# Decoding float64 weights with one VectorE operation fewer a half tile, the sign taken in by ScalarE, and the order planned with another TensorE rate

## The chip, the cores and the metric

One core of one Trainium2 chip runs the whole program. The metric is the device time of one execution in microseconds. Three executions of the kernel before took 681.01, 682.85 and 683.84 us; their median, 682.85 us, is the time that a change is measured against.

## The reference, cut to what matters

```python
def _attn_ref(q, k, v):                                  # 4 batches, 12 heads, 448 rows, 64 columns, float32
    scores = scale * np.matmul(q, k.transpose(0, 1, 3, 2))
    scores = np.where(mask, -1000000000.0, scores)       # causal
    scores = scores - np.max(scores, axis=-1, keepdims=True)
    attn = np.exp(scores)
    attn = attn / (np.sum(attn, axis=-1, keepdims=True) + 1e-09)
    return np.matmul(attn, v).astype(np.float32)

def _moe_ref(x, w_in, w_out):                            # x: 1792 x 768; w_in: 768 x 2048; w_out: 2048 x 768
    h = x @ w_in
    g = np.where(h >= 1, h, np.where(h <= -1, 0.0, (h + 1) ** 2 / 4.0))
    return (g @ w_out).astype(np.float32)
```

The attention's output, heads side by side, is the x of the two products behind it. The weights w_in and w_out arrive as float64: each is two 32-bit words, and the chip must make a float32 of them before TensorE can use it.

## The kernel before, in words

The work has three parts. **Attention** goes by 24 pairs of heads (4 batches of 6). For a pair, q and k are loaded and transposed on VectorE (line 446); scores are made on TensorE (lines 562, 567, 571); VectorE masks and takes the row bound (583); ScalarE takes the exponential (587); the rows are divided by their sum (510 to 513, GpSimd, ScalarE or VectorE); TensorE transposes them (525), and ScalarE copies them out (546); TensorE multiplies by v (612). **mlp1** makes h = x @ w_in for a batch of 448 rows and one of 16 blocks f of 128 columns, in 18 matmuls (line 405: 6 blocks of the sum, 3 passes of high and low parts); then comes the activation, written as min(r, 1) * max(h, r) with r = relu(h/2 + 1/2): ScalarE (414), VectorE (417), VectorE (419). The result goes to a scratch in HBM. A batch's blocks can be finished when all six pairs of that batch are done. **mlp2** reads the scratch back, splits it in high and low parts (325, 334), and makes the output in tiles of 128 rows with 3 passes for each block f (line 703).

The weights are decoded in halves of 128 x 384 weights by `decode` (line 341): 32 halves of w_in, then 32 of w_out, two for each f. The words of a half are loaded by SP's queue (line 360). The upper word, read as a float32, is multiplied by 2^-112, which moves the exponent's offset so that three bits can be dropped (line 361 on ScalarE, or line 363 on GpSimd); VectorE shifts it left by 3 (366), ors in the top three bits of the lower word (368), and ors in the sign bit of the upper word (371), which the shift has pushed out. The finished float32 is split: the high part is a rounding copy to the matmul's format (325, 327 or 326 on ScalarE, GpSimd or VectorE), the low part is the difference (334 or 335, GpSimd before VectorE). The buffer `wm` in which this happens has two slots, and a slot comes free when the low part of the half has been made. Weights share 16 slots `w`; w_out takes a slot when batch 3 of mlp1 has used that block of w_in.

The order of the instructions on each engine is not written by hand. `Plan.run` (line 105) simulates the engines, task by task, with a cost for each (lines 199 to 216, and `Clock` for TensorE, line 173): of the tasks that can start it takes the earliest, and among those on one engine the one of lower priority number. Where a task lists several engines, another one than the first is taken only if it would finish earlier than the first, counting what is queued on that (lines 125 to 134). `Clock.run` costs a matmul of n columns at n / 2.4 ns when TensorE is warm. The program is emitted in the order that the plan comes to, so a changed cost can move any instruction of the program. Attention has priority 13 for each pair (line 648), the decoding of block f of w_in has 80 + 3 f (line 645), mlp1's matmuls come behind all attention (line 654).

Of the kernel before, what the change touches and what calls it, by code (L numbers as in the profile page):

```python
# [10 lines left out]
F32 = mybir.dt.float32  # L11
F32R = mybir.dt.float32r
U32 = mybir.dt.uint32
ACTF = mybir.ActivationFunctionType
ALU = mybir.AluOpType
W_SHIFT = 2.0 ** -112


class Buf:
# [21 lines left out]
class Plan:  # L41
# [18 lines left out]
    def task(self, alts, prio, reads=(), writes=(), after=()):  # L60
        t = Task(alts, prio)
        for b, k in reads:
            w, rs = b.keys.setdefault(k, [None, []])
            if w is not None:
                t.deps.add(w)
            rs.append(t)
        for b, k in writes:
            w, rs = b.keys.setdefault(k, [None, []])
            if w is not None:
                t.deps.add(w)  # L70
            t.deps.update(r for r in rs if r is not t)
            b.keys[k] = [t, []]
        for b in {id(x): x for x, _ in (*reads, *writes)}.values():
            if not b.tasks and b.tag is not None:
                t.allocs.append(b)
            elif b.tasks and b.tag is not None:
                t.soft.add(b.tasks[0])
            b.tasks.append(t)
        t.deps.update(after)
        t.deps.discard(t)  # L80
        t.soft -= t.deps
        t.n_left = len(t.deps) + len(t.soft)
        for d in t.deps | t.soft:
            d.next.append(t)
        t.no = len(self.tasks)
        self.tasks.append(t)
        return t
# [85 lines left out]
class Clock:  # L173
# [7 lines left out]
    def run(self, t, matmuls):  # L181
        for n, m, rows, beside in matmuls:
            warm = self.cols.get(int(t / self.TICK) - 1, 0) >= self.ENOUGH
            d = max(m / 1.2, n / (2.4 if warm else 1.2)) / 1000 + (0.055 if beside else 0.002)
            a, z = int(t / self.TICK), int((t + d) / self.TICK)
            f = 1.0 if a == z else (z * self.TICK - t) / d
            self.cols[a] = self.cols.get(a, 0) + n * f * rows / 128
            self.cols[z] = self.cols.get(z, 0) + n * (1 - f) * rows / 128
            t += d
        return t  # L190


def mm(n, m=128, rows=128, times=1, pair=False):


    return [(n, m, rows, pair)] * times


def dve(n, fast=False):
    return ((n / 2 if fast else n) + 62) / 960  # L200


def act(n, extra=0.0):
    return n / 1200 + 0.055 + extra


def pool_ts(n, extra=0.0):
    return 0.83e-3 * n + 0.16 + extra


def pool_tt(n):
    return 2.08e-3 * n + 0.16


def dma(nbytes, rate=360.0):
    return nbytes / rate / 1000
# [3 lines left out]
def kernel(  # L220
# [9 lines left out]
    nc = tc.nc  # L230
    B, H, S, D = q.shape
# [24 lines left out]
    W2 = DM // 2  # L256
    scale = 1.0 / float(D) ** 0.5
# [29 lines left out]
    for z in range(2):  # L287
        nc.gpsimd.affine_select(
            out=mask[T * z:T * z + T, S - T:],
            in_=mask[T * z:T * z + T, S - T:],  # L290
# [9 lines left out]
        out=mask2[:, 2 * P:], in_=mask2[:, 2 * P:], pattern=[[-1, P]], compare_op=ALU.is_ge,  # L300
# [14 lines left out]
    task = plan.task  # L315

    def buf(tag, shape, dtype=F32):
        return plan.buf(tag, lambda: pools[tag].tile(shape, dtype, tag=tag, name=tag))

    def dma_task(out_fn, in_fn, cost, prio, **kw):  # L320
        return task([("SP", cost, lambda: nc.sync.dma_start(out=out_fn(), in_=in_fn()))], prio, **kw)  # L321
# [19 lines left out]
    def decode(w, c, src, prio, no):  # L341

        if no < 2 * (KF - NSTG):
            st, z = stages[no // 2 % NSTG], no % 2
            raw = lambda: st.tile.bitcast(U32)[:, z]
        else:
            st, z = buf("st", [P, 2 * S]), 0
            raw = lambda: st.tile.bitcast(U32)[:, :DM]
        m = buf("wm", [P, W2])

        def words(t):
            return raw().rearrange("p (c t) -> p c t", t=2)[:, :, t]

        def mu():
            return m.tile.bitcast(U32)

        hi = lambda: w[:, 0, c * W2:(c + 1) * W2]
        lo = lambda: w[:, 1, c * W2:(c + 1) * W2]
        dst, ap = src
        dma_task(lambda: dst(raw()), lambda: ap, dma(P * DM * 4), prio - 15, writes=[(st, (z, 0)), (st, (z, 1))])  # L360
        task([("ACT", act(W2, 0.04), lambda: nc.scalar.activation(
            out=m.tile, in_=words(1).bitcast(F32), func=ACTF.Copy, scale=W_SHIFT)),
              ("POOL", pool_ts(W2), lambda: nc.gpsimd.tensor_scalar(
            out=m.tile, in0=words(1).bitcast(F32), scalar1=W_SHIFT, scalar2=1.0, op0=ALU.mult, op1=ALU.mult))],
            prio, reads=[(st, (z, 1))], writes=[(m, 0)])
        task([("DVE", dve(W2, True), lambda: nc.vector.tensor_scalar(
            out=mu(), in0=mu(), scalar1=3, scalar2=None, op0=ALU.logical_shift_left))], prio, writes=[(m, 0)])
        task([("DVE", dve(W2), lambda: nc.vector.scalar_tensor_tensor(  # L368
            out=mu(), in0=words(0), scalar=29, in1=mu(), op0=ALU.logical_shift_right, op1=ALU.bitwise_or))],
            prio, reads=[(st, (z, 0))], writes=[(m, 0)])  # L370
        task([("DVE", dve(W2), lambda: nc.vector.scalar_tensor_tensor(  # L371
            out=mu(), in0=words(1), scalar=0x80000000, in1=mu(), op0=ALU.bitwise_and, op1=ALU.bitwise_or))],
            prio, reads=[(st, (z, 1))], writes=[(m, 0)])
        task(copy_alts(hi, lambda: m.tile, W2, "ACT POOL DVE"), prio, reads=[(m, 0)], writes=[(w, (0, c))])
        task(sub_alts(lo, lambda: m.tile, lambda: hi().bitcast(F32), W2, "POOL DVE"),
             prio, reads=[(m, 0), (w, (0, c))], writes=[(w, (1, c))])
# [21 lines left out]
    def mlp1(b, f, prio):  # L398
        h = buf("h", [P, 512])
        for kk in range(KD):  # L400
            x = XS[b, kk]

            def go(kk=kk, x=x):
                for n, (a, c) in enumerate(PASSES):
                    nc.tensor.matmul(  # L405
                        out=h[:, :S], lhsT=wi[f][:, a, kk * P:(kk + 1) * P], rhs=x[:, c],
                        start=(kk == 0 and n == 0), stop=(kk == KD - 1 and n == 2),
                    )

            task([("PE", mm(S, times=3), go)], prio,  # L410
                 reads=[(x, 0), (x, 1), (wi[f], (0, kk // K2)), (wi[f], (1, kk // K2))], writes=[(h, 0)])
        r, y = buf("r", [P, S]), buf("vv", [P, S])
        g0 = -1.0
        task([("ACT", act(S, 0.1), lambda: nc.scalar.activation(  # L414
            out=r.tile, in_=h[:, :S], func=ACTF.Relu, scale=0.5, bias=half[:, 0:1]))],
            g0, reads=[(h, 0)], writes=[(r, 0)])
        task([("DVE", dve(S), lambda: nc.vector.tensor_tensor(out=y.tile, in0=h[:, :S], in1=r.tile, op=ALU.max))],  # L417
             g0, reads=[(h, 0), (r, 0)], writes=[(y, 0)])
        task([("DVE", dve(S), lambda: nc.vector.scalar_tensor_tensor(  # L419
            out=r.tile, in0=r.tile, scalar=1.0, in1=y.tile, op0=ALU.min, op1=ALU.mult))],  # L420
            g0, reads=[(y, 0)], writes=[(r, 0)])
        dma_task(lambda: g_dram[f, :, b * S:(b + 1) * S], lambda: r.tile, dma(P * S * 4), g0,
                 reads=[(r, 0)], writes=[(gkeys, (f, b))])
# [222 lines left out]
    for b in range(B):  # L646
        for p in range(HP):
            prio = (b * HP + p) * 2 * HT
# [3 lines left out]
    for b in range(B):  # L652
        for f in range(KF):
            mlp1(b, f, 10000.0 + 1000 * b)
# [21 lines left out]
    for size in TILES:  # L676
        ts = list(range(tn, tn + size))
        t0, tn = tn, tn + size
        n = len(ts) * P
# [8 lines left out]
        for f in range(KF):  # L688
            prio = 6000.0 + t0 * 100 + f
# [3 lines left out]
                     prio, reads=[(gkeys, (f, b)) for b in bs], writes=[(raw, 0)], after=last)  # L693
            task(copy_alts(lambda gs=gs, n=n: gs[:, 0, :n], lambda raw=raw, n=n: raw[:, :n], n, "ACT POOL"), prio,
                 reads=[(raw, 0)], writes=[(gs, 0)])
            task(sub_alts(lambda gs=gs, n=n: gs[:, 1, :n], lambda raw=raw, n=n: raw[:, :n],
                          lambda gs=gs, n=n: gs[:, 0, :n].bitcast(F32), n, "DVE POOL"), prio,
                 reads=[(raw, 0), (gs, 0)], writes=[(gs, 1)])
            for t in ts:
# [9 lines left out]
                for steps in ([both[::2], both[1::2]] if f == KF - 1 else [both]):  # L709
                    task([("PE", mm(NO, times=len(steps)), lambda go=go, steps=steps: go(steps))],  # L710
                         20000.0 + t0 * 100 + f + 0.01 * t,
                         reads=[(gs, 0), (gs, 1)] + [(wo[f], x) for x in WK],
                         writes=[(acc[t, c], 0) for c in sorted({c for c, _ in steps})])
        for t in ts:
# [3 lines left out]
                out=ot[:, :NO], in_=a0[:, :NO], func=ACTF.Copy))], 0.0, reads=[(a0, 0)], writes=[(ot, 0)])  # L718
# [3 lines left out]
                out=ot[:, NO:cut], in_=a1[:, :cut - NO]))], 0.0, reads=[(a1, 0)], writes=[(ot, 1)])  # L722
            if final:
                task([("ACT", act(DM - cut), lambda ot=ot, a1=a1, cut=cut: nc.scalar.activation(
                    out=ot[:, cut:], in_=a1[:, cut - NO:NO], func=ACTF.Copy))], 0.0, reads=[(a1, 0)], writes=[(ot, 2)])
# [37 lines left out]
```

## Time and profile before

| | |
|---|---|
| median of three executions | 682.85 us (681.01 to 683.84) |
| the profiled execution, its own time | 683.23 us |
| its span, first to last instruction | 681.4 us |
| mean granted TensorE clock | 0.995 of full speed |

The profile shows one execution. Its own time is 1.8 us above its span and 0.4 us above the median. Times in the rows below are microseconds from the start of the span unless they say ns. PE is TensorE, DVE VectorE, ACT ScalarE, POOL GpSimd, SP the engine that issues all DMAs here. A busy matmul counts from its start to the end of its way through the array, so matmuls overlap in the records: the distance between starts tells how fast they go, and the busy time of an engine with short waits looks fuller than it is.

### The profile page before, as it was taken

How to read it: one execution, taken by the hardware profiler on the slowest of the kernel's cores; microseconds unless marked ns; L12 is line 12 of the kernel's file. 1: busy time of each engine (PE TensorE's matmuls, PEld its weight loads, DVE VectorE, ACT ScalarE, POOL GpSimd, SP SyncE). 2: the span in 40 equal slices, each digit the busy share in tenths (PEclk: the TensorE clock that was granted, in tenths of full speed). 3: DMA queues.
4: the chain of work that ended last, by engine and by line, in shares of the span. 5: the costliest groups of instructions: out<-in, count | busy, mean ns of one | idle time of the engine just before them, and what ended most of it. 6: DMA issues, size and time to landing. Idle time of an engine off the chain costs nothing.

```text
span 681.4 us, 11654 instructions
## 1 busy us (share of the span) xinstructions
PE 653.4 (96%) x3782; PEld 559.9 (82%) x3782; DVE 401.8 (59%) x922; ACT 314.0 (46%) x829; POOL 229.9 (34%) x369
## 2 busy tenths in 40 slices
PE   7988989898989999999999999999999999999997
PEld 3445767676767788777789789999999999999997
DVE  5667899999565666765665399887632112212221
ACT  3778766556556553775642544333422112111222
POOL 3257777676243333544330264353300000000000
PEclk8999999999989999999999999999999999999999
DMA  7668999985666666666674256566424212312312
GB/s 186 184 174 211 222 239 243 242 217 159 156 164 180 178 173 179 176 170 167 174 179 143 89 178 191 170 197 191 156 82 151 62 51 93 109 58 89 90 61 71
DMA packets 91900, 105.75 MB, mean 155 GB/s; under 512 B 34368, under 2 KB 75840, under 8 KB 91840
## 3 DMA queue, kind: packets, MB, share of 16 engines
q1 hardware_dynamic: 91840, 105.01, 56.2%
q8 instruction: 30, 0.49, 0.3%
q14 instruction: 30, 0.25, 0.1%
HBM read 67.35 MB, written 20.19 MB: 128 GB/s over the span
## 4 chain that ended last, share of the span: by engine, by line
PE 64%; DVE 12%; DMA 9%; issue 4%; POOL 3%; SPq 3%; ACT 3%; DVEq 0%; POOLq 0%; ACTq 0%
PE a L703 25%; PE h L405 16%; PE h L703 8%; PE t L612 5%; PE t L525 4%; SPq L321 3%; DMA st<-in_moe_w_out_dram 3%; DVE wm L368 3%; PE s L567 2%; DVE r L419 2%; DMA st<-in_k_dram 2%; PE s L562 2%; DVE wm L371 2%; DMA w<-in_moe_w_in_dram 2%; DMA st<-in_q_dram 1%
## 5 line engine op out<-in xcount | busy, mean ns | idle before, releaser
L405 PE MATMUL h<-x,w 128*128 128x448 f32 x1152 | 261.3, 372 | 2.6 <-POOL w L335 1.1
L405 PEld LDWEIGHTS h<-x,w 128*128 128x128 f32 x1152 | 209.2, 188 | 22.0 <-POOL w L335 2.3
L703 PE MATMUL a<-w,gs 128*128 128x384 f32 x1008 | 197.6, 334 | 0.0
L703 PEld LDWEIGHTS a<-w,gs 128*128 128x128 f32 x1008 | 176.8, 188 | 0.1
L334 DVE TENSOR_TENSOR gs<-gr,gs 128x512 fp32r<-128x512 f32 (+3 forms) x76 | 40.4, 532 | 137.5 <-ACT gs L325 137.5
L583 DVE CUSTOM_DVE_ANT_0 s<-s,mask 128x256 f32<-128x256 f32 (+6 forms) x168 | 73.0, 449 | 53.9 <-PE s L567 28.9
L325 ACT ACTIVATE gs<-gr 128x512 fp32r<-128x512 f32 (+3 forms) x79 | 39.2, 500 | 139.3 <-PE h L703 105.7
L587 ACT ACTIVATE e<-s,mn 128x256 f32<-128x256 f32 (+6 forms) x168 | 80.7, 487 | 40.2 <-DVE mn L583 36.5
L335 POOL TENSOR_TENSOR w<-wm,w 128x384 fp32r<-128x384 f32 x63 | 71.0, 1130 | 52.7 <-ACT w L325 51.1
L703 PE MATMUL h<-w,gs 128*128 128x384 f32 x336 | 80.8, 334 | 0.2 <-DVE vv L417 0.2
L510 POOL TENSOR_SCALAR e<-e,su 128x256 f32<-128x256 f32 (+5 forms) x103 | 64.1, 628 | 27.9 <-DVE su L598 19.3
L593 POOL TENSOR_SCALAR su<-su 128x2 f32<-128x2 f32 (+1 forms) x71 | 23.0, 325 | 135.7 <-ACT e L587 128.3
L525 PE MATMUL t<-ident,e 128*128 128x128 f32 x384 | 60.1, 281 | 8.8 <-POOL e L510 5.1
L546 ACT ACTIVATE pt<-t 128x384 f32<-128x384 f32 (+2 forms) x139 | 58.9, 464 | 19.0 <-PE t L525 18.2
L525 PEld LDWEIGHTS t<-ident,e 128*128 128x128 f32 x384 | 44.4, 142 | 26.2 <-POOL e L510 13.8
L703 PEld LDWEIGHTS h<-w,gs 128*128 128x128 f32 x336 | 60.2, 188 | 0.5 <-DVE vv L417 0.5
L414 ACT ACTIVATE r<-h,half 128x448 f32<-128x448 f32 x64 | 40.1, 630 | 39.1 <-PE h L405 38.5
L612 PE MATMUL t<-pt,vr 128*64 128x448 f32 (+3 forms) x384 | 52.0, 401 | 2.0 <-ACT pt L546 1.8
L417 DVE TENSOR_TENSOR vv<-h,r 128x448 f32<-128x448 f32 x64 | 39.5, 617 | 22.9 <-ACT r L414 22.7
L419 DVE SCALAR_TENSOR_TENSOR r<-r,vv 128x448 f32<-128x448 f32 x64 | 51.8, 810 | 0.9
L612 PEld LDWEIGHTS t<-pt,vr 128*64 128x64 f32 (+1 forms) x384 | 23.6, 138 | 34.4 <-issue 21.1
L446 DVE STREAM_TRANSPOSE qs<-st 128x448 f32<-128x448 f32 x48 | 46.3, 965 | 5.9 <-DMA st<-in_q_dram 3.4
(61 smaller groups left out, 563.2 us busy)
## 6 DMA issues: line engine op xcount, KB each, us to landing
g_scratch<-r SPq DMA_DIRECT2D x64, 224.0 KB, 2.2
st<-in_moe_w_out_dram SPq DMA_DIRECT2D x32, 384.0 KB, 3.2
w<-in_moe_w_in_dram SPq DMA_DIRECT2D x28, 384.0 KB, 5.2
st<-in_q_dram SPq DMA_DIRECT2D x96, 108.0 KB, 2.4
st<-in_k_dram SPq DMA_DIRECT2D x96, 108.0 KB, 2.6
q<-tt SPq DMA_DIRECT2D x76, 128.0 KB, 2.4
gr<-g_scratch SPq DMA_DIRECT2D x32, 256.0 KB, 2.7
k<-ks SPq DMA_DIRECT2D x76, 96.0 KB, 2.2
```

The lines of the kernel that those rows point to most:

```text
L334: "DVE": ("DVE", dve(n), lambda: nc.vector.tensor_tensor(out=dst(), in0=x(), in1=y(), op=op)),
L335: "POOL": ("POOL", pool_tt(n), lambda: nc.gpsimd.tensor_tensor(out=dst(), in0=x(), in1=y(), op=op)),
L405: nc.tensor.matmul(out=h[:, :S], lhsT=wi[f][:, a, kk * P:(kk + 1) * P], rhs=x[:, c], start=(kk == 0 and n == 0), stop=(kk == KD - 1 and n ...
L419: task([("DVE", dve(S), lambda: nc.vector.scalar_tensor_tensor(out=r.tile, in0=r.tile, scalar=1.0, in1=y.tile, op0=ALU.min, op1=ALU.mult)) ...
L446: task([("DVE", dve(S), lambda g=g, t=t: nc.vector.transpose(out=x[:, g].rearrange("p (r c) -> p c r", c=C), in_=t.tile.rearrange("p (c d) ...
L510: ("POOL", pool_ts(n, 0.09), lambda: nc.gpsimd.tensor_scalar(out=ev(), in0=ev(), scalar1=sc(), scalar2=1.0, op0=ALU.mult, op1=ALU.mult)),
L525: nc.tensor.transpose(t[:, c:c + P], es[i][:, j * P:(j + 1) * P], ident)
L546: task([("ACT", act(n), lambda: nc.scalar.activation(out=dst(), in_=src(), func=ACTF.Copy)), ("DVE", dve(n), lambda: nc.vector.tensor_copy ...
L583: task([("DVE", dve(n) + 0.01, lambda s=s, n=n, i=i: nc.vector.tensor_tensor_reduce(out=s[:, :n], in0=s[:, :n], in1=mask2[:, 3 * P - n:] i ...
L587: task([("ACT", act(n, 0.19), lambda s=s, n=n, i=i: nc.scalar.activation(out=es[i][:, :n], in_=s[:, :n], func=ACTF.Exp, scale=-1.0, bias=m ...
L612: nc.tensor.matmul(out=o[64 * g:64 * g + 64, j * P:S], lhsT=vr[:k, j, g, :], rhs=pt[:k, 7 * j:5 * j + NI, g, :], start=(j == 0), stop=(j = ...
L703: nc.tensor.matmul(out=acc[t, c][:, :NO], lhsT=gs[:, a, (t - t0) * P:(t - t0 + 1) * P], rhs=wo[f][:, z, c * NO:(c + 1) * NO], start=(f == ...
```

## The change

The scaling of the upper word becomes a Prelu on ScalarE with the same scale and a slope of 2^32 for negative words: these come out 2^32 times larger in magnitude, so the bit that the shift by 3 moves into the sign's place is set for them and clear for the others. The operation of line 371 is gone. The scaling can no longer go to GpSimd. In the plan, the or of line 368 costs 0.08 us more, a warm matmul n / 2.23 ns in place of n / 2.4 ns, and the last operation of the activation (419) may also go to GpSimd, there as two instructions.

```diff
--- before.py
+++ after.py
@@ -14,6 +14,7 @@
 ACTF = mybir.ActivationFunctionType
 ALU = mybir.AluOpType
 W_SHIFT = 2.0 ** -112
+W_SIGN = 2.0 ** 32
 
 
 class Buf:
@@ -181,7 +182,7 @@
     def run(self, t, matmuls):
         for n, m, rows, beside in matmuls:
             warm = self.cols.get(int(t / self.TICK) - 1, 0) >= self.ENOUGH
-            d = max(m / 1.2, n / (2.4 if warm else 1.2)) / 1000 + (0.055 if beside else 0.002)
+            d = max(m / 1.2, n / (2.23 if warm else 1.2)) / 1000 + (0.055 if beside else 0.002)
             a, z = int(t / self.TICK), int((t + d) / self.TICK)
             f = 1.0 if a == z else (z * self.TICK - t) / d
             self.cols[a] = self.cols.get(a, 0) + n * f * rows / 128
@@ -359,18 +360,13 @@
         dst, ap = src
         dma_task(lambda: dst(raw()), lambda: ap, dma(P * DM * 4), prio - 15, writes=[(st, (z, 0)), (st, (z, 1))])
         task([("ACT", act(W2, 0.04), lambda: nc.scalar.activation(
-            out=m.tile, in_=words(1).bitcast(F32), func=ACTF.Copy, scale=W_SHIFT)),
-              ("POOL", pool_ts(W2), lambda: nc.gpsimd.tensor_scalar(
-            out=m.tile, in0=words(1).bitcast(F32), scalar1=W_SHIFT, scalar2=1.0, op0=ALU.mult, op1=ALU.mult))],
+            out=m.tile, in_=words(1).bitcast(F32), func=ACTF.Prelu, scale=W_SHIFT, alpha=W_SIGN))],
             prio, reads=[(st, (z, 1))], writes=[(m, 0)])
         task([("DVE", dve(W2, True), lambda: nc.vector.tensor_scalar(
             out=mu(), in0=mu(), scalar1=3, scalar2=None, op0=ALU.logical_shift_left))], prio, writes=[(m, 0)])
-        task([("DVE", dve(W2), lambda: nc.vector.scalar_tensor_tensor(
+        task([("DVE", dve(W2) + 0.08, lambda: nc.vector.scalar_tensor_tensor(
             out=mu(), in0=words(0), scalar=29, in1=mu(), op0=ALU.logical_shift_right, op1=ALU.bitwise_or))],
             prio, reads=[(st, (z, 0))], writes=[(m, 0)])
-        task([("DVE", dve(W2), lambda: nc.vector.scalar_tensor_tensor(
-            out=mu(), in0=words(1), scalar=0x80000000, in1=mu(), op0=ALU.bitwise_and, op1=ALU.bitwise_or))],
-            prio, reads=[(st, (z, 1))], writes=[(m, 0)])
         task(copy_alts(hi, lambda: m.tile, W2, "ACT POOL DVE"), prio, reads=[(m, 0)], writes=[(w, (0, c))])
         task(sub_alts(lo, lambda: m.tile, lambda: hi().bitcast(F32), W2, "POOL DVE"),
              prio, reads=[(m, 0), (w, (0, c))], writes=[(w, (1, c))])
@@ -416,8 +412,13 @@
             g0, reads=[(h, 0)], writes=[(r, 0)])
         task([("DVE", dve(S), lambda: nc.vector.tensor_tensor(out=y.tile, in0=h[:, :S], in1=r.tile, op=ALU.max))],
              g0, reads=[(h, 0), (r, 0)], writes=[(y, 0)])
+        def pool_g():
+            nc.gpsimd.tensor_scalar(out=r.tile, in0=r.tile, scalar1=1.0, scalar2=1.0, op0=ALU.min, op1=ALU.mult)
+            nc.gpsimd.tensor_tensor(out=r.tile, in0=r.tile, in1=y.tile, op=ALU.mult)
+
         task([("DVE", dve(S), lambda: nc.vector.scalar_tensor_tensor(
-            out=r.tile, in0=r.tile, scalar=1.0, in1=y.tile, op0=ALU.min, op1=ALU.mult))],
+            out=r.tile, in0=r.tile, scalar=1.0, in1=y.tile, op0=ALU.min, op1=ALU.mult)),
+              ("POOL", pool_ts(S) + pool_tt(S), pool_g)],
             g0, reads=[(y, 0)], writes=[(r, 0)])
         dma_task(lambda: g_dram[f, :, b * S:(b + 1) * S], lambda: r.tile, dma(P * S * 4), g0,
                  reads=[(r, 0)], writes=[(gkeys, (f, b))])
```

## Rows read from the trace of the kernel before

**Rows 1.** The page: busy time, share of the span and instructions of each engine.

```profile
...
PE 653.4 (96%) x3782; PEld 559.9 (82%) x3782; DVE 401.8 (59%) x922; ACT 314.0 (46%) x829; POOL 229.9 (34%) x369
...
```

**Rows 2.** Stretches of the span: busy us of each engine, granted TensorE clock, DMA share, GB/s.

```profile
...
73.00:171.00 98.00, 87.86 (x485) 68.87 (x484) 93.70 (x200) 61.16 (x158) 71.30 (x88) 1.00 0.86 220
...
200.00:400.00 200.00, 199.05 (x1184) 163.45 (x1184) 122.86 (x318) 111.20 (x319) 71.47 (x136) 1.00 0.60 162
400.00:448.00 48.00, 46.96 (x234) 43.30 (x233) 42.88 (x71) 19.96 (x38) 20.24 (x19) 1.00 0.65 194
448.00:515.00 67.00, 66.81 (x386) 66.49 (x385) 43.25 (x63) 23.21 (x44) 21.95 (x23) 1.00 0.51 160
...
```

**Rows 3.** VectorE by line, 73 to 171 us: xcount | busy us, mean ns | idle.

```profile
...
L368 DVE SCALAR_TENSOR_TENSOR wm<-w,wm 128x384 uint32<-128x384 uint32 x25 | 17.8, 714 | 0.2
L371 DVE SCALAR_TENSOR_TENSOR wm<-w,wm 128x384 uint32<-128x384 uint32 x26 | 17.1, 659 | 0.1
...
L371 DVE SCALAR_TENSOR_TENSOR wm<-st,wm 128x384 uint32<-128x384 uint32 x4 | 2.4, 604 | 0.0
...
```

**Rows 4.** The chain of waits in the same stretch, shares by line.

```profile
...
by line: DVE wm L368 11.8%; DMA w<-in_moe_w_in_dram 10.7%; issue 9.1%; PE h L405 8.8%; DVE r L419 7.7%; DVE wm L371 7.3%; DMA vr<-in_v_dram 4.3%; DMA st<-in_q_dram 4.1%; DVE vv L417 4.0%; DVE wm L366 3.9%; DMA st<-in_k_dram 3.7%; DVE s L583
...
```

**Rows 5.** TensorE by line in the same stretch (columns as in group 3).

```profile
...
L405 PE MATMUL h<-x,w 128*128 128x448 f32 x280 | 65.0, 374 | 1.2 <-POOL w L335 1.1
L525 PE MATMUL t<-ident,e 128*128 128x128 f32 x68 | 10.9, 279 | 4.3 <-POOL e L510 3.7 <-ACT e L512 0.5
L612 PE MATMUL t<-pt,vr 128*64 128x448 f32 (+3 forms) x64 | 8.4, 391 | 0.0
L567 PE MATMUL s<-k,q 128*128 128x384 f32 (+1 forms) x32 | 6.7, 327 | 4.0 <-DMA q<-tt 1.8 <-DMA k<-ks 1.4 <-ACT e L587 0.6
...
```

**Rows 6.** The chain of waits of the whole span: start us, us, what.

```profile
...
213.30 0.91 PE t L525 x7
...
221.13 2.03 PE t L612 x16
...
357.51 16.42 PE h L405 x81
...
628.05 49.94 PE a L703 x288
```

**Rows 7.** TensorE by line, 200 to 400 us (columns as in group 3).

```profile
...
L405 PE MATMUL h<-x,w 128*128 128x448 f32 x598 | 137.3, 372 | 0.0
L525 PE MATMUL t<-ident,e 128*128 128x128 f32 x185 | 28.0, 276 | 0.5 <-POOL e L510 0.3
L612 PE MATMUL t<-pt,vr 128*64 128x448 f32 (+3 forms) x192 | 25.2, 391 | 0.0
L567 PE MATMUL s<-k,q 128*128 128x384 f32 (+1 forms) x88 | 19.0, 326 | 0.0
...
```

**Rows 8.** Line 371, whole span: duration min/median/max in ns, first and last start.

```profile
...
L371 DVE SCALAR_TENSOR_TENSOR wm<-st,wm x36: 540/557/1370, 157.2 to 495.1; 128x384 uint32<-128x384 uint32 x36
...
```

**Rows 9.** Timeline around 400 us: start us, us, engine, line.

```profile
...
399.90 1.31 POOL L335 TENSOR_TENSOR w<-wm,w 128x384 fp32r<-128x384 f32 x1 [1.79 <-ACT w L325]
400.26 1.37 DVE L371 SCALAR_TENSOR_TENSOR wm<-st,wm 128x384 uint32<-128x384 uint32 x1
...
```

**Rows 10.** Line 361 on ScalarE, 73 to 171 us: durations, and what ended its idle time.

```profile
...
L361 ACT ACTIVATE wm<-w x16: 538/558/567, 75.6 to 150.4; 128x384 f32<-128x384 f32 x16
...
  POOL w L335: 11.3, 8
...
```

**Rows 11.** Line 363, the same operation on GpSimd, 73 to 171 us.

```profile
...
L363 POOL TENSOR_SCALAR wm<-w x8: 528/645/812, 76.5 to 136.4; 128x384 f32<-128x384 f32 x8
...
```

**Rows 12.** By line and shape, whole span (columns as in group 3).

```profile
...
L327 POOL TENSOR_SCALAR tt<-qs 128x448 fp32r<-128x448 f32 x17 | 10.3, 607 | 16.6 <-DVE qs L446 14.8 <-DMA vr<-in_v_dram 0.9 <-DVE su L598 0.2
...
L335 POOL TENSOR_TENSOR tt<-qs,tt 128x448 fp32r<-128x448 f32 x8 | 9.2, 1152 | 0.6
...
L587 ACT ACT_TABLE_LOAD x1 | 1.3, 1283 | 0.7 <-PEq L747 0.7
...
```

## The prediction

> **What bounds the kernel now.** The page's shares come first: TensorE is busy for 96% of the span, VectorE for 59% [rows 1]. Taken alone that says that VectorE doesn't matter. The table by stretches says where it does. From 200 to 400 us TensorE lacks 0.95 us of 200, from 400 to 448 it lacks 1.04, from 448 to 515 it lacks 0.19; VectorE is at 61% in the first of these and at 89% in the second. From 73 to 171 us the picture is turned round: VectorE is busy 93.7 of 98 us, TensorE only 87.9, and the DMA engines are at 86% with 220 GB/s [rows 2]. In this stretch w_in is decoded and batch 0 of mlp1 runs as its blocks arrive.
>
> How much TensorE time is missing there is not its idle time, since matmuls overlap. I price them by runs of equal ones: 16.42 us for 81 gives 0.203 us for one of 448 columns, 49.94 for 288 gives 0.173 for one of 384, 0.91 for 7 gives 0.130 for a transpose, 2.03 for 16 gives 0.127 for one by v [rows 6]. In the slow stretch that is 280 x 0.203 = 56.8, 68 x 0.130 = 8.8, 64 x 0.127 = 8.1, 32 x 0.173 = 5.5, and 0.203 at most for the other 41 of the 485, 8.3: 87.5 us [rows 2, 5]. The same prices on the full stretch from 200 to 400 give 121.4 + 24.1 + 24.4 + 15.2, and 24.6 for the other 121 of 1184, 209.7 us where 200 passed [rows 2, 7]. So they are 5% too high, and the slow stretch holds about 83.5 us of TensorE work in 98: **14.5 us are to be had there at most**. The chain of waits says who has them: VectorE lines lead it (368 with 11.8%, 419 with 7.7%, 371 with 7.3%), and four loads, w_in the first, have 22.8% together [rows 4].
>
> **The removed operation.** Line 371 runs 64 times, once for each half. In the slow stretch there are 26 of 659 ns and 4 of 604 ns: 17.1 + 2.4 = 19.5 us of VectorE's 93.7 [rows 3]. That is not the gain. TensorE has 14.5 to give back. The DMA engines moved 220 GB/s at 86%; the same bytes at 100% would take 98 x 0.86 = 84.3 us, which leaves 13.7. And on the chain itself line 371 has 7.3% of 98 us, 7.2 us: what lies under it on the chain, another VectorE operation or a load, is next in line. I take 6 us, a little under that share, since loads have over a fifth of the chain and don't get faster. The ends are 0 (the loads were late anyway) and 13.7.
>
> The other 32 halves, of w_out, end at 495 us [rows 8]. They save about 32 x 0.6 = 19 us of VectorE time that nobody waits for: TensorE lacks 1.04 + 0.19 us from 400 to 515 [rows 2]. I take 0; the end is 1.2. The cover is mlp1's last batch, with VectorE at 42.9 of 48 us there; were decoding late there, each 0.6 us of it would show.
>
> **The scaling on ScalarE alone.** 16 of the scalings on ScalarE take a median of 558 ns; 8 on GpSimd take 645 [rows 10, 11]. Moving these gives ScalarE 8 x 0.56 = 4.5 us more, 65.7 of 98, and takes 5.2 from GpSimd's 71.3 [rows 2]: both have room, so 0. No row shows a Prelu. Below it can't be under the 538 ns minimum of the scaling now; above I bound it by the slowest scaling of the stretch, 812 ns, 30 x 0.25 = 7.6 us more on an engine with 32 spare. I take 558, the same operand and size. What the move does add is a wait at the head of ScalarE's queue: a scaling needs a `wm` slot, which GpSimd's low part frees; 8 times ScalarE stood 11.3 us in all for that [rows 10], with exponentials and copies of the transposes queued behind it. On GpSimd that wait didn't exist, since it makes the low parts itself. Eight more such waits are 11 us; I expect them to fall in ScalarE's slack, since VectorE, not ScalarE, then feeds the attention, and take 0, with 11 as the end.
>
> **The activation's last step.** On GpSimd it would be a tensor_scalar and a tensor_tensor at 607 + 1152 ns [rows 12], and hold the only `vv` slot. The plan takes GpSimd only where VectorE's queue stands over a microsecond later than GpSimd's; the step has nearly the first priority, and none of VectorE's tasks costs more than (448 + 62) / 960 = 0.53 us in the plan (line 200), so this should be rare: 0.
>
> **The plan's rate and the 0.08.** These cost nothing on the chip; they permute the order. The measured 0.203 us for 448 columns [rows 6] is 2.21 columns a ns, so the plan now sees TensorE as it is, and should put fewer fillers ahead of attention's links. From 200 to 400 only 0.95 us are there to be won [rows 2]; nearest for a bad order is the slow stretch, where 4.3 us of idle time stand before transposes and 4.0 before scores [rows 5]. I take 0 with ends of -4 and +8.
>
> **Sum:** 683.23 us, the profiled execution's own time, minus 6 gives 677.2 (rounded). That execution lies 0.4 above the median of 682.85, so I state **676.9**.
>
> The trace shows 371 at 540 ns at best and at 1.37 us where it starts during GpSimd's low part, which is then at 1.31 [rows 8, 9]. The Trainium skill, "SBUF — State Buffer", section "Who interferes with whom", has for this that a VectorE instruction with two SBUF inputs and a GpSimd instruction that reads SBUF lock each other out for a whole instruction. By that rule the removed operation would also stop holding up GpSimd's low parts, and the sum would go to the last rival below instead of the 676.9 that the chain's share gives. The rows agree that the two hold each other up at that meeting, but with a mean of 659 ns against 540 at best [rows 3, 8] not that this is the usual case.
>
> **The rivals.**
>
> *The loads hold it.* Four loads have 22.8% of the chain, three times line 371's share [rows 4]. If decoding then waits for w_in, at most 2 us come back: 681.2, 680.9 against the median. Against it: 86% is not full, and VectorE has only 4.3 us idle in 98 [rows 2]. Chance 0.18.
>
> *ScalarE stands for wm slots: slower.* The eight moved scalings wait like the eight that waited, 11.3 us, ahead of exponentials. If that falls on attention's chain, 677.2 + 11.3 = 688.5, 688.1 against the median. It decides where more than half of it, 6 us, is not covered. For it: ScalarE's waits for GpSimd's low parts are already there. Against: ScalarE is idle 37 of 98 us [rows 2]. Chance 0.14.
>
> *Table loads: slower.* The one table load of the program took 1283 ns [rows 12]. If a Prelu and an exponential don't share a table, about 30 scalings among exponentials bring up to 60 loads, 77 us on ScalarE with 32 spare: some 45 us, 728. Nothing in the trace speaks for it but that no Prelu was there before. The Trainium skill, "ScalarE: Activation LUTs", section "Table sets: the hidden batching unit", says that functions are loaded by named sets and that cheap ones are in every set, without naming Prelu. Chance 0.04.
>
> *All of it comes back.* Line 371 held up GpSimd's low parts as well [rows 9], and these held `wm` and with it the next half; both go at once, and the stretch shortens to the loads' 84.3 us: 683.2 - 13.7 = 669.5, 669.1 against the median. For it: a meeting costs line 371 up to 1.37 - 0.54 = 0.83 us. Against it: the mean exceeds the best by 0.12 us only. Chance 0.06. The forecast itself, 3.5 to 10 us gained, has 0.58.
>
> **Numbers.** About 0.5%, 3.4 us, is what a measurement of this kernel can tell from no change. Faster by more: 0.58 + 0.06 = 0.64. Within: the loads, 0.18. Slower by more: 0.14 + 0.04 = 0.18. The range goes from 668, which holds the full gain, to 687, which holds the loads and about half of the waiting rival; outside stay the table loads, the rest of the waits and a few hundredths below.
>
> **What would show it.** Right: line 371's group is missing; VectorE from 73 us to the end of decoding w_in falls well under 95%, that decoding ends some 6 us sooner, and TensorE's idle time before 200 shrinks while the stretch from 400 on is as long as before. The loads: w_in's transfers lead the chain there. The waits: ScalarE's idle time before the scaling, released by GpSimd's low part, doubles. Table loads: their count. I am wrong on the order if TensorE's idle time between 200 and 400 us, now 0.95, grows by more than 2.

## The result, and the profile after

The changed kernel takes 685.88 us (median of nine, 683.42 to 690.07) against 682.37 for the kernel before in nine runs beside it: ratio 1.0059, 95% interval 1.0039 to 1.008. It is slower, by about half a per cent, though VectorE has 38 us less to do. The profiled execution took 688.48 us, its span is 686.7, 5.3 longer than before. First the page after:

```profile
span 686.7 us, 11569 instructions
...
PE 656.4 (96%) x3782; PEld 565.0 (82%) x3782; DVE 363.8 (53%) x873; ACT 321.3 (47%) x842; POOL 197.4 (29%) x341
```

Then the stretches of the span after, with the columns of [rows 2] (busy us of TensorE, weight loads, VectorE, ScalarE and GpSimd, granted clock, DMA share, GB/s):

```profile
0.00:73.00 73.00, 66.04 (x422) 38.42 (x423) 48.16 (x157) 51.49 (x158) 35.37 (x87) 0.98 0.73 191
73.00:171.00 98.00, 83.99 (x445) 66.04 (x444) 80.16 (x176) 61.92 (x162) 58.35 (x81) 0.95 0.88 223
171.00:200.00 29.00, 28.96 (x186) 22.84 (x187) 20.00 (x59) 20.98 (x61) 9.28 (x21) 1.00 0.74 188
200.00:400.00 200.00, 196.08 (x1162) 160.81 (x1158) 116.08 (x308) 109.20 (x309) 58.25 (x120) 1.00 0.58 157
400.00:448.00 48.00, 47.59 (x228) 43.92 (x229) 33.78 (x57) 21.64 (x42) 19.21 (x17) 0.96 0.69 210
448.00:515.00 67.00, 65.55 (x377) 65.08 (x376) 29.86 (x47) 21.92 (x42) 16.48 (x16) 1.00 0.43 128
```

The relief came: from 73 to 171 us VectorE falls from 93.70 us to 80.16, and GpSimd from 71.30 to 58.35. TensorE does less in this stretch, 445 matmuls where 485 ran before, but that is not yet the loss. The rows on either side of it in the kernel before:

```profile
0.00:73.00 73.00, 62.42 (x407) 35.64 (x408) 49.40 (x158) 49.79 (x157) 36.82 (x90) 0.98 0.75 191
...
171.00:200.00 29.00, 27.28 (x155) 19.52 (x154) 16.06 (x46) 15.96 (x46) 8.09 (x18) 0.94 0.61 152
```

By 200 us the changed kernel has run 422 + 445 + 186 = 1053 matmuls and the kernel before 407 + 485 + 155 = 1047. The mix differs a little: 22 + 246 + 64 = 332 against 10 + 280 + 56 = 346 of mlp1's, the dearest, and 20 more of the others; so the two are about level. The time is lost behind that: from 200 to 515 us TensorE stands idle for 3.92 + 0.41 + 1.45 = 5.78 us, where it was 0.95 + 1.04 + 0.19 = 2.18 before, 3.6 us more. The clock of 0.96 from 400 to 448 us, 1.00 before, is worth at most another 48 x 0.04 = 1.9 us, an estimate. Together that is about the 5.3 us of the longer span. The stretch from 200 to 400 us, full before, grew by 2.97 us of idle time: the sign by which the prediction said it would be wrong on the order.

The groups by line after, whole span (xcount | busy us, mean ns | idle before, releaser):

```profile
L419 DVE SCALAR_TENSOR_TENSOR r<-r,vv 128x448 f32<-128x448 f32 x64 | 43.3, 676 | 1.1
...
L367 DVE SCALAR_TENSOR_TENSOR wm<-st,wm 128x384 uint32<-128x384 uint32 x36 | 24.4, 679 | 0.8
L367 DVE SCALAR_TENSOR_TENSOR wm<-w,wm 128x384 uint32<-128x384 uint32 x28 | 20.1, 718 | 0.4
L362 ACT ACTIVATE wm<-st 128x384 f32<-128x384 f32 x36 | 19.7, 548 | 19.5 <-DMA st<-in_moe_w_out_dram 15.0 <-POOL w L336 1.5 <-DVE w L335 1.4
L362 ACT ACTIVATE wm<-w 128x384 f32<-128x384 f32 x28 | 15.4, 555 | 3.4 <-POOL w L336 3.3
...
L588 ACT ACT_TABLE_LOAD x1 | 1.3, 1283 | 0.7 <-PEq L748 0.7
```

Line 371 and its 64 operations are gone. The Prelu takes 548 to 555 ns, as the scaling did [rows 10], there is still one table load, and ScalarE's wait for `wm` slots, freed by the low parts, is 3.3 + 1.5 + 1.4 = 6.2 us, not 11.3. All 64 last steps of the activation are on VectorE: the choice of GpSimd is never taken, and the program planned without that choice has the same instructions in the same order on every engine. So every part of the change that issues something does what it says, and what is left is the order.

The chain of waits after, 73 to 171 us, to be held against [rows 4]:

```profile
by line: PE h L401 19.2%; DMA q<-tt 11.4%; DMA st<-in_k_dram 9.7%; issue 7.8%; DMA st<-in_q_dram 6.2%; DMA k<-ks 5.5%; DMA g_scratch<-r 4.3%; PE s L568 4.0%; DVE r L419 3.9%; DVE wm L367 3.8%; PE t L613 3.0%; PE t L526 2.6%; DVE wm L365 2.1
```

VectorE's decoding has left the front; mlp1's matmuls and transfers have taken it.

### The profile page after: what moved, and what is told of

The parts are those of the page before. It is cut to its first block, busy times and chain, and to the rows that moved or that the text cites. A ratio compares the mean times of both kernels' runs of the same rounds, so it can differ in the third digit from the quotient of the medians.

```text
span 686.7 us, 11569 instructions
## 1 busy us (share of the span) xinstructions
PE 656.4 (96%) x3782; PEld 565.0 (82%) x3782; DVE 363.8 (53%) x873; ACT 321.3 (47%) x842; POOL 197.4 (29%) x341
## 4 chain that ended last, share of the span: by engine, by line
PE 63%; DVE 11%; DMA 11%; issue 4%; SPq 4%; ACT 4%; POOL 3%; DVEq 0%; ACTq 0%; POOLq 0%
PE a L704 25%; PE h L401 18%; PE h L704 8%; SPq L322 4%; PE t L613 4%; PE t L526 3%; DMA st<-in_k_dram 3%; DMA st<-in_moe_w_out_dram 2%; PE s L568 2%; DMA st<-in_q_dram 2%; DVE qs L447 2%; DVE wm L367 2%; DMA q<-tt 2%; DVE wm L365 2%; DVE r L419 2%
## 5 line engine op out<-in xcount | busy, mean ns | idle before, releaser
L401 PE MATMUL h<-x,w 128*128 128x448 f32 x1152 | 264.2, 376 | 2.2 <-DVE vv L413 2.2
L401 PEld LDWEIGHTS h<-x,w 128*128 128x128 f32 x1152 | 212.2, 191 | 21.5 <-DVE vv L413 2.9
L335 DVE TENSOR_TENSOR gs<-gr,gs 128x512 fp32r<-128x512 f32 (+3 forms) x79 | 44.2, 560 | 153.3 <-ACT gs L326 151.3
L336 POOL TENSOR_TENSOR w<-wm,w 128x384 fp32r<-128x384 f32 x62 | 69.1, 1118 | 60.0 <-ACT w L326 58.4
L511 POOL TENSOR_SCALAR e<-e,su 128x256 f32<-128x256 f32 (+6 forms) x102 | 58.2, 577 | 28.2 <-DVE su L599 22.3
L547 ACT ACTIVATE pt<-t 128x256 f32<-128x256 f32 (+2 forms) x139 | 60.0, 467 | 12.8 <-PE t L526 11.3
L594 POOL TENSOR_SCALAR su<-su 128x2 f32<-128x2 f32 (+1 forms) x72 | 20.5, 285 | 146.7 <-ACT e L588 142.5
L365 DVE TENSOR_SCALAR wm<-wm 128x384 uint32<-128x384 uint32 x64 | 35.1, 549 | 19.8 <-ACT wm L362 19.3
```

Source lines behind the costliest of these rows:

```text
L335: "DVE": ("DVE", dve(n), lambda: nc.vector.tensor_tensor(out=dst(), in0=x(), in1=y(), op=op)),
L336: "POOL": ("POOL", pool_tt(n), lambda: nc.gpsimd.tensor_tensor(out=dst(), in0=x(), in1=y(), op=op)),
L401: nc.tensor.matmul(out=h[:, :S], lhsT=wi[f][:, a, kk * P:(kk + 1) * P], rhs=x[:, c], start=(kk == 0 and n == 0), stop=(kk == KD - 1 and n ...
L511: ("POOL", pool_ts(n, 0.09), lambda: nc.gpsimd.tensor_scalar(out=ev(), in0=ev(), scalar1=sc(), scalar2=1.0, op0=ALU.mult, op1=ALU.mult)),
L547: task([("ACT", act(n), lambda: nc.scalar.activation(out=dst(), in_=src(), func=ACTF.Copy)), ("DVE", dve(n), lambda: nc.vector.tensor_copy ...
```

## The experiments

The runs come in four sets, each timed beside the kernel before, which took 680.98 to 682.16 us (median) in them and 682.37 beside the changed kernel. A difference in us between kernels of different sets is therefore good to about 1 us; the ratios take that out.

**The removal alone, in the old order.** The plan keeps the old tasks and costs. Where ScalarE scales (50 of 64 halves), the Prelu is issued and the sign's operation is not; the 14 halves that the plan gives to GpSimd stay as they were. In the cuts of the edits here, `...` marks what is left out, and the comments behind # are added.

```diff
+        task([("ACT", act(W2, 0.04), scale_act),                  # Prelu, notes it in `signed`
               ("POOL", pool_ts(W2), lambda: nc.gpsimd.tensor_scalar(
...
-        task([("DVE", dve(W2), lambda: nc.vector.scalar_tensor_tensor(
+        task([("DVE", dve(W2), sign)], prio, reads=[(st, (z, 1))], writes=[(m, 0)])   # issues nothing if `signed`
```

> The plan is the old one, costs and order unchanged on every engine; where ScalarE does the scaling (50 of 64 halves) it is a Prelu and the sign's VectorE operation is not issued; the other 14 halves are decoded as before. Theory A (the removed operation is worth its share of the chain, and the new order gives it back): 3 to 7 us faster than before, ratio 0.990 to 0.996, with VectorE well under 95% from 73 to 171 us. Theory B (VectorE's relief is worth nothing there, since loads hold the stretch): within 0.3% of before, ratio 0.997 to 1.003, VectorE's freed time turned into waits for loads.

675.43 us against 681.53, ratio 0.9918 (0.9891 to 0.9946): 6.1 us faster, as forecast for the part. Its stretches, same columns; its chain of waits from 73 to 171 us; and what is left there of the sign's operation (xcount | busy us, mean ns):

```profile
73.00:171.00 98.00, 89.88 (x501) 71.31 (x501) 87.48 (x183) 62.88 (x163) 69.24 (x89) 1.00 0.84 224
...
400.00:448.00 48.00, 48.00 (x241) 44.28 (x240) 37.91 (x59) 19.95 (x38) 18.81 (x20) 1.00 0.61 197
```

```profile
by line: DMA w<-in_moe_w_in_dram 22.8%; PE h L414 9.2%; issue 8.4%; DVE wm L379 7.2%; DMA st<-in_moe_w_in_dram 6.3%; DMA st<-in_k_dram 4.6%; SPq L322 3.5%; ACT r L423 3.2%; DVE qs L455 2.9%; POOL w L336 2.5%; PE t L534 2.5%; DMA k<-ks 2.3%;
```

```profile
L370 DVE SCALAR_TENSOR_TENSOR wm<-w,wm 128x384 uint32<-128x384 uint32 x9 | 6.6, 735 | 0.0
L370 DVE SCALAR_TENSOR_TENSOR wm<-st,wm 128x384 uint32<-128x384 uint32 x1 | 0.5, 548 | 0.0
```

501 matmuls in the stretch, 16 more than before, and the loads of w_in now lead the chain with 22.8 + 6.3 = 29.1%. Ten of the sign's operations are still there, so it is some 20 fewer, 19.5 - 7.1 = 12.4 us of VectorE's time, that bought the 6 us; the loads stood next on the chain.

**The other corner: the new order with the old decode.** The sign's operation follows the or again, in all 64 halves; `join` issues both. The scaling stays on ScalarE in all of them.

```diff
-            out=m.tile, in_=words(1).bitcast(F32), func=ACTF.Prelu, scale=W_SHIFT, alpha=W_SIGN))],
+            out=m.tile, in_=words(1).bitcast(F32), func=ACTF.Copy, scale=W_SHIFT))],
...
-        task([("DVE", dve(W2) + 0.08, lambda: nc.vector.scalar_tensor_tensor(
+        task([("DVE", dve(W2) + 0.08, join)], prio, reads=[(st, (z, 0)), (st, (z, 1))], writes=[(m, 0)])   # the or, then the sign
```

> The new order on every engine, but the sign's VectorE operation is put back behind the or in all 64 halves, and the scaling is a plain copy with a scale again. Theory A: 3 to 9 us slower than the changed kernel, 689 to 695 us, ratio to before 1.010 to 1.019. Theory B: as the changed kernel, ratio 1.003 to 1.009.

704.1 us, ratio 1.0339 (1.0309 to 1.0369). In the new order the removal is worth 704.1 - 685.88 = 18.2 us; the new order costs 704.1 - 681.53 = 22.6 us with the old decode. Both effects are larger than I wrote, and they nearly cancel in the change.

**Each part planned anew.** The decode edit alone at 2.4 (without the 0.08 and the GpSimd choice), and the rate alone, whose whole edit is:

```diff
-            d = max(m / 1.2, n / (2.4 if warm else 1.2)) / 1000 + (0.055 if beside else 0.002)
+            d = max(m / 1.2, n / (2.23 if warm else 1.2)) / 1000 + (0.055 if beside else 0.002)
```

> The decode edit alone, planned anew at the old rate of 2.4, without the 0.08 and without the GpSimd choice for the activation. Theory A, if the rate made the order bad: 3 to 7 us faster than before, ratio 0.990 to 0.996. Theory A, if any new order loses against the old one: 682 to 688, ratio 0.999 to 1.008. Theory B: ratio 0.998 to 1.008 and loads ahead on the chain of waits from 73 to 171 us.

> The old decode, planned with 2.23 in place of 2.4. If the rate is what makes the order bad: 3 to 10 us slower than before, ratio 1.004 to 1.015, with TensorE's clock at its lower level more often than in the kernel before (its record there: two stretches of 3.4 us). If the rate is harmless and the decode edit is at fault: within 0.3% of before.

The decode edit alone: 678.67 us, ratio 0.9967 (0.9949 to 0.9986), 2.9 us faster and just short of the 3 to 7 expected. The rate alone: 700.53 us, ratio 1.0296 (1.0265 to 1.0328), nearly twice the most that I wrote. Its stretches, and TensorE's waits for `vv` over the whole span (us in total, times, longest):

```profile
0.00:73.00 73.00, 61.70 (x401) 34.33 (x402) 50.14 (x157) 50.51 (x157) 37.16 (x88) 0.98 0.71 188
73.00:171.00 98.00, 83.92 (x448) 64.27 (x446) 92.94 (x196) 57.02 (x148) 71.99 (x93) 0.97 0.76 210
171.00:200.00 29.00, 28.13 (x168) 22.52 (x167) 17.70 (x42) 15.54 (x42) 8.12 (x16) 1.00 0.69 184
200.00:400.00 200.00, 197.47 (x1176) 160.25 (x1175) 118.17 (x323) 112.92 (x324) 62.73 (x125) 1.00 0.59 160
400.00:448.00 48.00, 43.84 (x211) 38.73 (x210) 41.85 (x65) 19.51 (x39) 21.45 (x21) 1.00 0.56 173
448.00:515.00 67.00, 63.71 (x351) 62.72 (x350) 47.31 (x70) 22.80 (x45) 25.94 (x25) 0.97 0.51 156
```

```profile
PE h L405 <- DVE vv L417: 4.2, 4, 1.9
PE h L703 <- DVE vv L417: 3.3, 1, 3.3
```

At 200 us it is 30 matmuls behind the kernel before (401 + 448 + 168 = 1017), and from 200 to 515 us TensorE stands idle for 2.53 + 4.16 + 3.29 = 9.98 us, where that had 2.18. Most of this is in the two stretches from 400 us on, in which w_out is decoded: there TensorE waits 4.2 + 3.3 = 7.5 us for `vv`, 1.2 in the kernel before.

**Why should an exact rate make a bad order?** Theory C: the plan's other engines (its helpers, as I call VectorE and GpSimd here) are too cheap as well, and making TensorE alone exact tips the balance. Theory D: any new order is a draw in a lottery. First four runs: the changed kernel at 2.4; without the 0.08; the new decode at 2.6; and at 2.23 with the helpers charged more:

```diff
 def dve(n, fast=False):
-    return ((n / 2 if fast else n) + 62) / 960
+    return ((n / 2 if fast else n) + 62) / 960 + 0.08
 def pool_ts(n, extra=0.0):
-    return 0.83e-3 * n + 0.16 + extra
+    return 0.83e-3 * n + 0.28 + extra
 def pool_tt(n):
-    return 2.08e-3 * n + 0.16
+    return 2.08e-3 * n + 0.28
```

> The changed kernel planned with the old rate of 2.4, the 0.08 on the or kept. Theory C (the plan's engines must be wrong by like amounts: its VectorE and GpSimd costs are too low, so a TensorE made exact alone looks late and gets its inputs late): 4 to 10 us faster than the changed kernel, 676 to 682, ratio to before 0.992 to 1.000. Theory D (orders are a lottery, each small change of a cost draws anew): anywhere from 675 to 700, without regard to the rate.

> The changed kernel with the rate of 2.23 and the or of the decode at its old plan cost. Theory C: 2 to 12 us slower than the changed kernel, 688 to 698, since the 0.08 mends a part of what the rate breaks. Theory D: anywhere from 675 to 700.

> The new decode planned with 2.6, no 0.08. Theory C: no worse than at 2.4, which took 678.7: 674 to 680. Theory D: anywhere from 675 to 700.

> The new decode planned with 2.23, and each VectorE task 0.08 us and each GpSimd task 0.12 us dearer in the plan, near what the rows show. Theory C: the loss at 2.23 goes, 674 to 682, ratio 0.989 to 1.000. Theory D: anywhere from 675 to 700.

In this last run the or goes without its own 0.08. Then the mirror (the same edit at 2.4 with the opposite signs), the helpers dearer at 2.4, and two more rates of the changed kernel:

> The mirror of the last run: the new decode planned with 2.4, each VectorE task 0.08 us and each GpSimd task 0.12 us cheaper in the plan than they were. Theory C (it is the balance between the engines in the plan, and TensorE too dear against VectorE and GpSimd is what costs): 684 to 700, ratio 1.004 to 1.028. Theory D (a lottery of orders, in which 2.23 happened to lose three times): anywhere from 674 to 700, and if the rate itself is the cause, 674 to 680.

> The new decode planned with 2.4, VectorE and GpSimd tasks dearer by 0.08 and 0.12 us. Theory C: no worse than with 2.4 alone, 670 to 680. Theory D: anywhere from 674 to 700.

> The changed kernel planned with 2.3, between 2.4, which took 674.2, and 2.23, which took 685.9. Theory C: between them, 675 to 685. Theory D: anywhere from 674 to 700.

> The changed kernel planned with 2.1, slower than the chip's own rate. Theory C: worse than at 2.23, 686 to 705, ratio 1.007 to 1.035. Theory D: anywhere from 674 to 700.

Last, which of the helpers, and how far it goes:

> The new decode planned with 2.23, VectorE's tasks 0.08 us dearer, GpSimd's as they were. If VectorE's plan cost is what counts: 674 to 680, as with both (675.3). If GpSimd's is: 684 to 690, as with neither (687.4). If both: between, 679 to 684.

> The new decode planned with 2.23, GpSimd's tasks 0.12 us dearer, VectorE's as they were. If VectorE's plan cost is what counts: 684 to 690. If GpSimd's is: 674 to 680. If both: between, 679 to 684.

> The new decode planned with 2.6, VectorE's and GpSimd's tasks dearer by 0.08 and 0.12 us. If the gain goes on with the balance: 664 to 671, below 669.6. If it has an optimum near 2.4 with these costs: 670 to 678.

All with the new decode; the last column is the ratio to before with its interval:

| rate | VectorE, GpSimd in the plan | us | ratio |
|---|---|---|---|
| 2.1 | or + 0.08 | 699.27 | 1.0261 (1.0243 to 1.028) |
| 2.23 | or + 0.08 (the change) | 685.88 | 1.0059 (1.0039 to 1.008) |
| 2.3 | or + 0.08 | 681.71 | 1.0002 (0.9988 to 1.0016) |
| 2.4 | or + 0.08 | 674.18 | 0.9903 (0.9879 to 0.9927) |
| 2.23 | as before | 687.43 | 1.009 (1.0069 to 1.0111) |
| 2.4 | as before (decode alone) | 678.67 | 0.9967 (0.9949 to 0.9986) |
| 2.6 | as before | 675.3 | 0.9922 (0.9898 to 0.9946) |
| 2.4 | 0.08, 0.12 cheaper | 692.12 | 1.015 (1.0131 to 1.017) |
| 2.23 | 0.12 dearer on GpSimd only | 680.85 | 0.9983 (0.9964 to 1.0003) |
| 2.23 | 0.08 dearer on VectorE only | 676.39 | 0.9918 (0.989 to 0.9946) |
| 2.23 | 0.08, 0.12 dearer | 675.28 | 0.9916 (0.9888 to 0.9944) |
| 2.6 | 0.08, 0.12 dearer | 672.27 | 0.9853 (0.9827 to 0.9879) |
| 2.4 | 0.08, 0.12 dearer | 669.63 | 0.9829 (0.9797 to 0.9862) |

Theory C's directions came. With the 0.08 the four rates stand in order, 25 us from one end to the other. Cheapening the helpers at 2.4 costs 13.5 us, though the rate is the good one; charging them at 2.23 wins back 12.2, though the rate is the bad one. Of the two, VectorE's cost counts for more (11.0 us alone) than GpSimd's (6.6 alone), and they don't add. What the 0.08 on the or does at 2.23 (687.43 against 685.88) is not clear of the noise.

The seven kernels that charge all helpers alike can be put in one row by a proportion of the plan: its cost of an or (0.465, 0.385 or 0.545 us) over its cost of a matmul of 448 columns (448 / rate + 2 ns). At 2.04, 2.29, 2.46, 2.67, 2.68, 2.89 and 3.12 they take 692.12, 687.43, 678.67, 675.3, 675.28, 669.63 and 672.27 us. On the chip the mean or of the slow stretch is 0.714 / 0.203 = 3.5 such matmuls [rows 3, 6]. A lottery would not line up like that, though there is some of it: the last step up is no gain, and at 2.1, where the other VectorE tasks stand near 2.16 by this count, 699.27 us is out of the row. Nor is the best plan the one with each cost nearest to the chip: that is 2.23 with the helpers dearer, 5.6 us behind 2.4 with the helpers dearer.

The expectations missed in size three times: at 2.4 the changed kernel was faster than I wrote, without the 0.08 a little less slow, and the helpers dearer at 2.4 a little faster. That last kernel, 669.63 us, beats both kernels of this case.

**How the order loses, seen at one place.** The timeline of the changed kernel's VectorE from 395.59 us (start us, us, engine, line):

```profile
395.59 1.45 DVE L365 TENSOR_SCALAR wm<-wm 128x384 uint32<-128x384 uint32 x1
396.96 0.98 DVE L335 TENSOR_TENSOR gs<-gr,gs 128x512 fp32r<-128x512 f32 x1
397.87 1.35 DVE L367 SCALAR_TENSOR_TENSOR wm<-st,wm 128x384 uint32<-128x384 uint32 x1
399.14 0.68 DVE L335 TENSOR_TENSOR gs<-gr,gs 128x512 fp32r<-128x512 f32 x1
399.74 0.61 DVE L413 TENSOR_TENSOR vv<-h,r 128x448 f32<-128x448 f32 x1
```

The same stretch on GpSimd, ScalarE and TensorE (in brackets the idle time before, and its releaser):

```profile
395.22 1.60 POOL L336 TENSOR_TENSOR gs<-gr,gs 128x512 fp32r<-128x512 f32 x1
...
396.10 0.62 ACT L410 ACTIVATE r<-h,half 128x448 f32<-128x448 f32 x1
...
397.49 1.31 POOL L336 TENSOR_TENSOR w<-wm,w 128x384 fp32r<-128x384 f32 x1
...
400.41 1.11 PE L401 MATMUL h<-x,w 128*128 128x448 f32 x2 [2.23 <-DVE vv L413]
```

Lines 365 and 367, the shift and the or, take less where no GpSimd operation runs beside them, a few us later on VectorE:

```profile
402.59 0.35 DVE L365 TENSOR_SCALAR wm<-wm 128x384 uint32<-128x384 uint32 x1
...
403.39 0.55 DVE L367 SCALAR_TENSOR_TENSOR wm<-st,wm 128x384 uint32<-128x384 uint32 x1
```

The r that `vv` needs is there at 396.72 (396.10 + 0.62). Four other VectorE operations stand ahead of `vv` in the order; the plan charges them 0.265 + 0.598 + 0.545 + 0.598 = 2.0 us, the chip takes 4.15 (395.59 to 399.74), most of the excess where they meet GpSimd's operations. So `vv` starts 3.0 us after its r is there, the `h` buffer comes free that much later, and TensorE stands still for 2.23. A plan that has TensorE exact and VectorE at half of what such a stretch takes can put work ahead of `vv` that it believes to be over in time. The Trainium skill, "SBUF — State Buffer", section "Who interferes with whom", has it that a VectorE operation with two SBUF inputs, or in a two-port mode, and a GpSimd operation that reads SBUF shut each other out: the one that comes second is blocked until the first is done. The or's 1.35 us beside GpSimd's 1.31 agrees, against 0.55 us later; so does the shift's 1.45 beside 1.60, against 0.35, if it is in such a mode, which no row shows.

The changed kernel's two waits of TensorE for `vv`, over the whole span:

```profile
PE h L401 <- DVE vv L413: 2.2, 1, 2.2
...
PE h L704 <- DVE vv L413: 1.4, 1, 1.4
```

Summed like this, the wait is 2.8 to 8.1 us in each of the six kernels that take over 685 us, and 1.6 or less in each of the eight under 679; the three between have 0.6 to 2.7. So it goes with the loss. It does not make up all of it (3.6 us here, where the kernel before had 1.2), and that each of these waits comes about like the one above is argued, not shown.

**The clock, a part of the price.** The changed kernel has a granted clock of 0.988 in the mean, against 0.995 before, and 0.95 in the slow stretch. The stretches around its three falls there (columns as above):

```profile
86.10:89.50 3.40, 1.30 (x8) 0.85 (x6) 2.42 (x9) 1.17 (x4) 1.79 (x2) 1.00 0.80 226
89.50:92.90 3.40, 3.37 (x13) 2.89 (x14) 2.46 (x8) 2.94 (x10) 2.90 (x7) 0.51 0.55 129
103.20:106.60 3.40, 0.92 (x5) 0.51 (x3) 3.37 (x5) 1.22 (x2) 2.73 (x4) 1.00 1.13 191
106.60:110.00 3.40, 3.32 (x12) 3.11 (x13) 2.07 (x9) 1.53 (x4) 0.48 (x1) 0.50 1.08 266
120.30:123.70 3.40, 1.50 (x9) 1.01 (x8) 3.40 (x6) 2.33 (x7) 2.43 (x3) 1.00 0.50 134
123.70:127.10 3.40, 3.40 (x11) 1.54 (x11) 3.18 (x8) 2.21 (x6) 1.34 (x3) 0.50 0.87 242
```

Of TensorE's two levels, 2.4 and 1.2 GHz, the second row of each pair has the lower one; in the first row TensorE was busy for only 1.30, 0.92 and 1.50 us. The place above does the same: behind its 2.23 us of idle time the clock falls (the kernel before has 1.00 from 400 to 448 us [rows 2]):

```profile
400.00:410.00 10.00, 9.59 (x40) 8.82 (x41) 6.45 (x13) 4.28 (x9) 2.93 (x3) 0.83 0.78 249
```

So a gap costs more than itself: here 2.23 us and, as an estimate, another 10 x 0.17 = 1.7. The three falls of the slow stretch leave the changed kernel about level at 200 us. And the clock does not separate these kernels: the changed kernel at 2.4 has 0.990 in the mean and is 11.7 us faster, and the one without the 0.08 has 0.998 and is no faster than the change. The clock follows the gaps.

## Why the prediction was wrong, point by point

**What bounds the kernel, and the removed operation:** right. I took 6 us, out of line 371's 7.3% of the chain; the old order without it gives 6.1, with 50 of the 64 removed. The loads were next, as said. The nothing for w_out's halves holds in the old order; in the new one, which is late there, the removal is worth some 18 us in all.

**The scaling on ScalarE, the activation's last step, the table:** right, all at nothing. The rival with ScalarE's waits did not come (6.2 us in place of 11.3), nor the table loads. The bound of 0.53 us on VectorE's plan costs was wrong (the difference of 512 columns is planned at 0.598), but GpSimd was never chosen all the same.

**The plan's rate and the 0.08:** this step failed. I wrote that an exact TensorE "should put fewer fillers ahead of attention's links", took 0 and gave it the ends -4 and +8. The rate alone costs 19.0 us with the old decode (700.53 against 681.53) and 11.7 with the new one (685.88 against 674.18, 10.6 by the two ratios); the 0.08 gives back 4.5 at 2.4, and nothing clear of the noise at 2.23. The sum is then -6 or more for the decode, some +11 for the rate: slower. The sign that I named for this, over 2 us more idle time from 200 to 400 us, came with 2.97. Two readings would have warned me. I compared one engine's plan cost with the chip and not the others': line 368 is planned at 0.465 us and took 0.714 there [rows 3], GpSimd's difference of 384 is planned at 0.96 and takes over 1.1. TensorE at 2.4 was 7% too cheap in the plan, its helpers some 15 to 55% by these two, so the exact rate moved the plan away from the chip's proportions. And I priced the order by what TensorE had idle in the good stretch, which bounds the gain, not the loss. How that order turns into waits is seen at one place and in the `vv` waits of all kernels; where the rest of the lost time comes from stays open.

**The range and the chances:** 668 to 687 holds the 685.88 by luck: the room above was left for the waits of a rival that didn't come. Slower had 0.18. The mechanism that made it slower was not among the rivals.

## What to carry to other kernels

Where a plan's costs set the order, it is their proportions that matter: making one engine exact while the others stay too cheap can lose more than the edit gains, so try the proportion itself, and charge an engine nearer to what it takes in company than to what it takes alone. Before an edit is judged together with a new order, run it in the old order (issue nothing for the removed task and keep its cost): here that parted -6 us from some +10, by the ratios 0.9918 and 1.0059. In this case a freed operation was worth its share of the chain down to the next link, not its busy time.

## What was not expected of the hardware

Two VectorE operations that take 0.35 and 0.55 us a few us later took 1.45 and 1.35 us beside GpSimd, close to the length of the GpSimd operations (1.60 and 1.31 us) that ran then. I had put such meetings down as rare by the mean of 659 ns. Two in a row cost 1.9 us here, as an estimate, of the 3.0 us that `vv` came after its r, and TensorE stood still for 2.23. Behind it the granted clock was 0.83 from 400 to 410 us.
